# Attention products in plain float32, queries on partitions, inside a fused attention and MoE kernel

## The chip, the cores and the metric

The kernel runs on one core of one Trainium2 chip. The metric is device time of one execution in microseconds (us). Engines are named as the profile names them: PE (TensorE; PEld its weight loads), DVE (VectorE), ACT (ScalarE), POOL (GpSimd), SP (SyncE, which issues all DMAs).

## The reference

Sixteen heads (B = 2, H = 8) of 576 queries, D = 64, feed two dense stages over 1152 tokens:

```python
scores = scale * q @ k.T                        # causal
a = softmax(scores); local = a @ v              # the sum gets + 1e-9
q_p = where(q > 0, q, exp(q) - 1) + 1           # phi
mem_out = (q_p @ M_prev) / (q_p @ z_prev + 1e-6)
attn = g * mem_out + (1 - g) * local            # g = sigmoid(beta[h])
x = attn as (1152, 512)
x = ((x @ w1) * (x @ w2)) @ w3 @ w_out          # these four arrive as float64
out = sum over e of p[:, e] * (relu(x @ e_w1[e]) @ e_w2[e])   # 4 experts
```

## The kernel before, in words

Products are made accurate by splitting each operand into a high part rounded to the matrix type `float32r` and a low part (value minus high), and adding two or three float32r products (`PASSES`, line 29). A split costs a rounding copy (`hi`) and a subtraction (`lo`) on ACT, DVE or POOL (lines 75 to 82).

The program has four stretches. **Attention** goes head by head in slots of `run_slot(n)` (line 406): slot n holds the splits of head n+2 (`stage_h`), the scores and exponentials of head n+1 (`stage_a`), the transposes and value products of head n (`stage_b`), and for each pair of heads phi (`stage_pa`) and its transpose (`stage_pb`). The 576 queries are five tiles of 120 rows that start 114 apart; tile i sees 120, 234, 348, 462 or 576 keys. **Fills** run in the same slots: `wo_unit` converts w_out from float64 (8 units), `w_unit` converts w3 and multiplies it with w_out into W (16 units, tiles `w3s`, `wacc`), `b0` converts w1 and w2 and makes `ab` and `hT` for the first 576 tokens (16 units, tiles `ws`, `asb`), and `c_unit` multiplies `hT` by W (tiles `c`, `x2a`). Then comes **the second half of the tokens** (`b1`, lines 633 to 643: the same two steps), and last **the experts** (lines 663 to 711, products `d` and `o`).

In attention a score product is two float32r matmuls of 128 rows (both halves of a split stacked on partitions). DVE adds the mask and takes the row minimum (line 278), ACT makes the exponential and its row sum (line 284), POOL and ACT scale the probabilities by the gate over the sum (line 331). PE transposes the blocks of P (line 367), ACT and DVE split them (`ph`, `pl`), and the value and memory products accumulate with queries along columns (`xv`). phi is computed with queries on partitions, normalised, then transposed.

A float64 conversion (`from64`) reads a 512 KB raw tile, takes three DVE operations (lines 101, 102, 105) and one on ACT; raw tiles have two buffers, so load u+2 waits for unit u's last read.

What sets the order: the lists of times `PA_AT` to `B_AT` order the steps inside a slot, `WO_SLOTS`, `W_SLOTS` and `B_SLOTS` place the fills, and a scheduler then fixes one static order for each engine. Engines run their order strictly and wait on semaphores; the experts cannot start before `x2a` is there.

Of the kernel before, what the change touches and what calls it, by code (L numbers as in the profile page):

```python
# [10 lines left out]
U32 = mybir.dt.uint32  # L11
AF = mybir.ActivationFunctionType
# [20 lines left out]
def kernel(  # L33
    ctx: ExitStack,
    tc: tile.TileContext,
    q: bass.AP,
# [16 lines left out]
    B, H, S, D = q.shape  # L53
# [78 lines left out]
    raw_t, split_t, prob_t, xraw_t = {}, {}, {}, {}  # L132
    pair_t, pT_t = {}, {}
    ms2 = [A1.tile([P, 2, 2 * D], F32R, name=f"ms{i}") for i in range(2)]
    for t in ms2:
        nc.gpsimd.memset(r32(t), 0.0)

    def load_pair(p):

        b, h = divmod(2 * p, H)  # L140
        qn = A1.tile([RP, NQ, 2, D], F32, tag="qn", name=f"qn{p}")
        for x in range(2):
            src = q[b, h + x]
            nc.sync.dma_start(out=qn[:, :, x, :], in_=bass.AP(src.tensor, src.offset, [[D, RP], [R * D, NQ], [1, D]]))
        z = A1.tile([P, 2 * D], F32, tag="z", name=f"z{p}")
        nc.sync.dma_start(
            out=z, in_=z_prev[b, h : h + 2].rearrange("h d -> (h d)").unsqueeze(0).to_broadcast([P, 2 * D])
        )
        mr = A1.tile([P, D], F32, tag="mr", name=f"mr{p}")
        nc.sync.dma_start(out=mr, in_=M_prev[b, h : h + 2].rearrange("h d e -> (h d) e"))  # L150
        pair_t[p] = {"q": qn, "z": z, "m": mr}

    def load_head(n):

        b, h = divmod(n, H)
        ts = []
        for nm, src in (("q", qT), ("k", kT)):
            t = A1.tile([P, S], F32, tag=f"{nm}d", name=f"{nm}d{n}")
            for x in range(2):
                nc.sync.dma_start(out=t[x * D : (x + 1) * D, :], in_=src[b, h])  # L160
            ts.append(t)
        t = A2.tile([RP, NQ, D], F32, tag="vr", name=f"vr{n}")
        x = v[b, h]
        nc.sync.dma_start(out=t, in_=bass.AP(x.tensor, x.offset, [[D, RP], [R * D, NQ], [1, D]]))
        raw_t[n] = (*ts, t)

    def stage_pa(p):
# [3 lines left out]
        st = pair_t[p]
        h = 2 * p % H

        def phi_a():
            st["ex"] = ex = st["q"]
            st["phi"] = phi = A1.tile([RP, NQ, 2, D], F32, tag="phi", name=f"phi{p}")
            nc.scalar.activation(phi, st["q"], AF.Relu)
            nc.scalar.activation(ex, st["q"], AF.Exp)
            nc.vector.scalar_tensor_tensor(out=phi, in0=ex, scalar=1.0, in1=phi, op0=ALU.min, op1=ALU.add)

        def phi_b():
            ex, phi = (st[x].rearrange("p n h d -> p n (h d)") for x in ("ex", "phi"))
            nc.gpsimd.tensor_mul(ex, phi, st["z"][0:RP].unsqueeze(1).to_broadcast([RP, NQ, 2 * D]))
            m = ms2[p % 2]
            for x in range(2):
                o = slice(x * D, (x + 1) * D)
                hi_pool(m[o, x, 0:D], st["m"][o, :])
                lo_pool(m[o, x, D:], st["m"][o, :], m[o, x, 0:D])

        def phi_c():  # L190
            st["nrm"] = nrm = A1.tile([RP, NQ, 2], F32, tag="nrm", name=f"nrm{p}")
            nc.vector.reduce_sum(out=nrm, in_=st["ex"], axis=AX.X)
            nc.vector.scalar_tensor_tensor(
                out=nrm, in0=nrm, scalar=1e-6, in1=gm[0:RP, h : h + 2].unsqueeze(1).to_broadcast([RP, NQ, 2]),
                op0=ALU.add, op1=ALU.mult,
            )
            nc.vector.reciprocal(nrm, nrm)

        def phi_d():
            phi = st["phi"]  # L200
            nc.vector.tensor_mul(phi, phi, st["nrm"].unsqueeze(3).to_broadcast([RP, NQ, 2, D]))
# [7 lines left out]
    def stage_pb(p):  # L209

        if p >= B * H // 2:
            return []
        st = pair_t.pop(p)
        pT = A2.tile([P, 2, S], F32R, tag="pT", name=f"pT{p}")
        pT_t[2 * p] = pT_t[2 * p + 1] = pT

        def trans(c0, c1):
            def f():
                t0, t1 = q0[c0], q0[c1 - 1] + rows[c1 - 1]
                ps = psQ.tile([P, 512], F32, tag="Q", name=f"tp{c0}_{p}")[:, 0 : t1 - t0]  # L220
                for c in range(c0, c1):
                    w = rows[c]
                    nc.tensor.transpose(
                        ps[:, q0[c] - t0 : q0[c] - t0 + w], st["phi"][0:w, c].rearrange("p h d -> p (h d)"),
                        identF[0:w, 0:w],
                    )
                nc.scalar.copy(pT[:, 0, t0:t1], ps)
                lo_dve(pT[:, 1, t0:t1], ps, pT[:, 0, t0:t1])
            return f

        return [*zip(PB_AT, (trans(0, NQ - 1), trans(NQ - 1, NQ)))]

    def stage_h(n):

        if n >= B * H:
            return []
        qd, kd, vr = raw_t.pop(n)
        T = A2.tile([P, S], F32R, tag="T", name=f"T{n}")
        K = A2.tile([P, 2, S], F32R, tag="K", name=f"K{n}")
        vs = A2.tile([RP, NQ, 2 * D], F32R, tag="vs", name=f"vs{n}")  # L240
        split_t[n] = T, K, vs

        def fq():
            nc.scalar.copy(T, qd)
            lo_pool(T[D : 2 * D, :], qd[D : 2 * D, :], T[D : 2 * D, :])

        def fk():
            nc.scalar.copy(K[:, 0, :], kd)
            lo_pool(K[:, 1, :], kd, K[:, 0, :])

        def fv():
            hi_pool(vs[:, :, 0:D], vr)
            lo_pool(vs[:, :, D:], vr, vs[:, :, 0:D])

        def nothing():
            pass

        return [*zip(H_AT, (fk, fq, nothing, fv))]

    def stage_a(n):  # L260
# [61 lines left out]
        def norm():  # L322
            nc.vector.tensor_scalar(
                out=sm, in0=sm, scalar1=1e-9, scalar2=gl[0:RP, h : h + 1], op0=ALU.add, op1=ALU.mult
            )
            nc.vector.reciprocal(sm, sm)  # L326
            for i in range(NQ):
                if i == NQ - 1:
                    nc.scalar.activation(Pt[i], Pt[i], AF.Copy, scale=sm[:, i : i + 1])
                else:  # L330
                    nc.gpsimd.tensor_scalar(  # L331
                        out=Pt[i], in0=Pt[i], scalar1=sm[:, i : i + 1], scalar2=1.0, op0=ALU.mult, op1=ALU.mult
                    )

        return [
            *zip(A_AT, (s0, s1, s2, s3, norm))
        ]

    QC = 2 * R
    QH = ((0, QC), (QC, S))  # L340
    offs = [S * j - R * j * (j - 1) // 2 for j in range(NQ)]
# [405 lines left out]
```

## Time and profile before

| | us |
|---|---|
| median of 3 executions (802.13 to 914.89) | 803.92 |
| the profiled execution | 803.4 |
| its span, first to last instruction | 801.6 |
| PE busy in the span | 739.9 |
| DVE, POOL, ACT busy | 397.8, 354.3, 286.2 |

The shares of the whole span are means over stretches with different limits, so the stretches have to be read apart. A busy PE is an overlapping count: matmuls are pipelined, and the distance from one start to the next is what a matmul costs.

### The profile page before, as it was taken

What the parts mean: (1) busy time and instruction counts of PE and PEld (TensorE: products, weight loads), DVE (VectorE), ACT (ScalarE), POOL (GpSimd) and SP (SyncE); (2) the same over time, 40 slices, a digit from 0 to 9 for tenths busy, and PEclk for the clock granted to TensorE, in tenths of its full rate; (3) what the DMA queues carried; (4) which work ended last, traced back from release to release, by engine and by line L of the source; (5) the groups of instructions that cost most, each with busy time, mean ns of one, the idle gap of its engine ahead of it and who ended that gap; (6) DMA issues with size and microseconds to landing.
All of it is one profiled execution on the core that took longest, in us unless ns stands there. A gap on an engine that the chain in (4) does not pass through costs nothing.

```text
span 801.6 us, 11092 instructions
## 1 busy us (share of the span) xinstructions
PE 739.9 (92%) x4120; PEld 655.6 (82%) x4120; DVE 397.8 (50%) x786; ACT 286.2 (36%) x639; POOL 354.3 (44%) x362
## 2 busy tenths in 40 slices
PE   3768688899899999989999999999999999999998
PEld 2656577679798999889988988889888898888986
DVE  5999988989999962756331211212112121121211
ACT  5777667667777733343220101201012010120100
POOL 7998987686754325723392009500095001600000
PEclk9666899989999999999999999999999999999999
DMA  7634445454342322531141003200033000201010
GB/s 195 180 115 139 136 140 151 127 152 133 117 118 86 105 80 80 170 106 54 28 130 54 1 1 119 92 1 1 1 121 90 1 1 1 66 0 40 14 40 26
DMA packets 65477, 64.37 MB, mean 80 GB/s; under 512 B 25360, under 2 KB 50960, under 8 KB 65424
## 3 DMA queue, kind: packets, MB, share of 16 engines
q1 hardware_dynamic: 65424, 63.67, 26.6%
q8 instruction: 32, 0.52, 0.3%
q14 instruction: 21, 0.17, 0.1%
HBM read 61.30 MB, written 2.36 MB: 79 GB/s over the span
## 4 chain that ended last, share of the span: by engine, by line
PE 63%; DVE 17%; POOL 6%; DMA 6%; issue 5%; ACT 3%; SPq 0%; DVEq 0%; POOLq 0%; ACTq 0%
PE d L673 25%; PE o L690 25%; PE ab L508 4%; PE c L568 4%; PE wacc L456 2%; DMA wr<-in_moe_w_dram 2%; DVE tu L102 2%; DMA w3r<-in_moe_w3T_dram 2%; DVE tf L105 2%; DVE P L278 2%; POOL P L331 2%; DVE pl L82 2%; PE xv L391 1%; DMA qd<-in_qT_dram 1%; PE pt L367 1%
## 5 line engine op out<-in xcount | busy, mean ns | idle before, releaser
L690 PE MATMUL o<-el,he 128*128 128x512 f32 x864 | 201.3, 393 | 0.0
L690 PEld LDWEIGHTS o<-el,he 128*128 128x128 f32 x864 | 161.9, 188 | 36.4
L679 ACT ACTIVATE he<-d 128x512 fp32r<-128x512 f32 (+2 forms) x96 | 47.2, 491 | 342.4 <-PE d L673 339.9
L76 POOL TENSOR_SCALAR el<-rel 128x512 fp32r<-128x512 f32 x64 | 40.4, 636 | 210.8 <-PE d L673 187.8
L680 DVE SCALAR_TENSOR_TENSOR he<-d,he 128x512 fp32r<-128x512 f32 (+2 forms) x96 | 53.5, 558 | 147.8 <-ACT he L679 147.8
L508 PE MATMUL ab<-xT,ws 128*128 128x288 f32 x768 | 115.7, 302 | 1.9 <-DVE asb L555 1.6
L673 PE MATMUL d<-x2b,el 128*128 128x384 f32 (+1 forms) x768 | 113.7, 309 | 0.0
L673 PEld LDWEIGHTS d<-x2b,el 128*128 128x128 f32 x768 | 113.1, 189 | 0.7
L508 PEld LDWEIGHTS ab<-xT,ws 128*128 128x128 f32 x768 | 107.5, 193 | 3.6 <-DVE asb L555 1.6
L673 PE MATMUL d<-x2a,el 128*128 128x512 f32 x384 | 89.6, 394 | 0.0
L673 PEld LDWEIGHTS d<-x2a,el 128*128 128x128 f32 x384 | 72.1, 188 | 16.7
L79 POOL TENSOR_TENSOR el<-rel,el 128x512 fp32r<-128x512 f32 x64 | 83.5, 1319 | 1.6
L699 DVE SCALAR_TENSOR_TENSOR acc<-o,pr,acc 128x512 f32<-128x512 f32 x27 | 20.3, 751 | 125.7 <-PE o L690 125.7
L273 PE MATMUL sc<-K,T 128*120 128x120 f32 (+2 forms) x192 | 49.7, 382 | 18.4 <-POOL K L79 10.9
L456 PE MATMUL wacc<-wo,w3s 128*128 128x512 f32 x192 | 55.4, 439 | 6.3 <-DVE W L82 6.3
L568 PE MATMUL c<-hT,W 128*128 128x288 f32 x384 | 56.0, 297 | 3.3 <-DVE hT L82 3.1
L331 POOL TENSOR_SCALAR P<-P,sm 120x120 f32<-120x120 f32 (+1 forms) x64 | 48.8, 778 | 20.6 <-DVE sm L326 13.2
L568 PEld LDWEIGHTS c<-hT,W 128*128 128x128 f32 x384 | 52.1, 188 | 4.3 <-DVE hT L82 3.8
L273 PEld LDWEIGHTS sc<-K,T 128*120 128x120 f32 x192 | 34.6, 225 | 23.9 <-POOL K L79 11.4
L284 ACT ACTIVATE P<-P,mn 120x120 f32<-120x120 f32 (+4 forms) x80 | 46.6, 583 | 19.4 <-DVE mn L278 19.0
L456 PEld LDWEIGHTS wacc<-wo,w3s 128*128 128x128 f32 x192 | 40.0, 215 | 15.4 <-DVE W L82 7.0
L367 PE MATMUL pt<-identF,P 114*120 114x114 f32 (+1 forms) x240 | 43.8, 297 | 8.5 <-POOL P L331 5.5
(89 smaller groups left out, 966.7 us busy)
## 6 DMA issues: line engine op xcount, KB each, us to landing
wr<-in_moe_w_dram SPq DMA_DIRECT2D x32, 512.0 KB, 3.4
rel<-in_moe_w_dram SPq DMA_DIRECT2D x64, 256.0 KB, 2.7
w3r<-in_moe_w3T_dram SPq DMA_DIRECT2D x16, 512.0 KB, 3.5
qd<-in_qT_dram SPq DMA_DIRECT2D x32, 144.0 KB, 3.7
kd<-in_kT_dram SPq DMA_DIRECT2D x32, 144.0 KB, 3.1
wor<-in_moe_w_out_dram SPq DMA_DIRECT2D x8, 512.0 KB, 3.7
vr<-in_v_dram SPq DMA_DIRECT2D x16, 150.0 KB, 3.0
qn<-in_q_dram SPq DMA_DIRECT2D x16, 150.0 KB, 3.8
```

The lines of the kernel that those rows point to most:

```text
L79: nc.gpsimd.tensor_sub(dst, src, r32(hi))
L273: nc.tensor.matmul(ps_ap, lhsT=T[:, q0[i] : q0[i] + RP], rhs=K[:, 1 - m, k0:k1], start=(m == 0), stop=(m == 1))
L284: nc.scalar.activation(Pt[i], Pt[i], AF.Exp, bias=mn[:, i : i + 1], scale=-1.0, accum_out=sm[:, i : i + 1])
L331: nc.gpsimd.tensor_scalar(out=Pt[i], in0=Pt[i], scalar1=sm[:, i : i + 1], scalar2=1.0, op0=ALU.mult, op1=ALU.mult)
L367: nc.tensor.transpose(pt[:, o - c0 : o - c0 + rows[i]], Pt[i][0 : rows[i], q0[j] : q0[j] + RP], identF[0 : rows[i], 0 : rows[i]],)
L456: nc.tensor.matmul(wacc[t], lhsT=w3s[u][:, a, c, :], rhs=wo[4 * g + c][:, bb, :], start=(g == 0 and c == 0 and x == 0), stop=(g == 1 and c ...
L508: nc.tensor.matmul(ps[:, 0:HS], lhsT=self.ws[u][:, wi, kk, :], rhs=xT[b, kk][:, xi, a * HS : (a + 1) * HS], start=(n == 0), stop=(n == 3 * ...
L568: nc.tensor.matmul(st["ps"][:, 0:HS], lhsT=Wt[kk][:, wi, d * P : (d + 1) * P], rhs=hT[kk][:, xi, a * HS : (a + 1) * HS], start=(kk == 0 an ...
L673: nc.tensor.matmul(ps, lhsT=ew1[m // 4 * 4 + kk][:, wi, m % 4 * P : (m % 4 + 1) * P], rhs=rhs[:, xi, :], start=(n == 0), stop=(n == 3 * KD ...
L679: nc.scalar.activation(ht[:, 0, :], ps, AF.Relu)
L680: nc.vector.scalar_tensor_tensor(out=ht[:, 1, :], in0=ps, scalar=0.0, in1=r32(ht[:, 0, :]), op0=ALU.max, op1=ALU.subtract,)
L690: nc.tensor.matmul(po, lhsT=hs[kk][:, xi, tt * P : (tt + 1) * P], rhs=ew2[kk][:, wi, :], start=(n == 0), stop=(n == 3 * KF - 1),)
```

## The change

The attention products become plain float32 instead of sums of float32r products, with queries on partitions in the results. Scores: one product of 64 rows (`qd`, `kd` as loaded, two heads of a pair on the two halves of the partitions). Values and memory: the transposed block of P (or phi, now computed on the transposed q) is the stationary operand, and v (or M) is the moving one with a column of ones (or z) beside it, so the row sum comes out as column 65; the result is scaled by gate over sum on DVE (`out_of`) and the two parts are added on POOL. The finished pair is transposed and split into `xT`. The splits of q, k, v, P, M and phi are gone, as are the scaling of P and the plain `q` input. In `from64` the shift on DVE becomes an ACT operation on the upper 16 bits of the low word. The `hi` copies of w_out, w3 and b0's weights move from ACT to POOL, b0's `lo` from DVE to POOL. The lists of times are new, and the fills start earlier: `wo_unit` from slot -0.8, `w_unit` in slots 1 to 8, `b0` in 8 to 13, `c_unit` in 13 to 16.

```diff
-WO_SLOTS = (0, 0, 0, 1, 1, 1, 2, 2)
-W_SLOTS, B_SLOTS = (3.0, 10.5), (10.5, 15.0)
+WO_SLOTS = (-0.8, -0.5, -0.2, 0.1, 0.3, 0.5, 0.7, 0.9)
+W_SLOTS, B_SLOTS, C_SLOTS = (1.0, 8.0), (8.0, 13.0), (13.0, 16.0)
 def from64(raw, tmp, nm):
+        nc.scalar.activation(u, raw.bitcast(U16)[..., 1], AF.Copy, scale=2.0**-13, bias=2.0**-14 - 0.5)
         nc.scalar.activation(t, hi.bitcast(F32), AF.Copy, scale=2.0**-112)
-        nc.vector.tensor_scalar(out=u, in0=lo, scalar1=29, scalar2=None, op0=ALU.logical_shift_right)
 def load_pair(p):
...
+            t = A2.tile([P, S], F32, tag=f"{nm}d", name=f"{nm}d{p}")
+            nc.sync.dma_start(out=t, in_=src[b, h : h + 2].rearrange("h d s -> (h d) s"))
 def stage_phi(p):
...
+            nc.gpsimd.tensor_scalar(out=phi, in0=qd, scalar1=0.0, scalar2=1.0, op0=ALU.max, op1=ALU.mult)
+            nc.scalar.activation(ex, qd, AF.Exp)
+            nc.vector.scalar_tensor_tensor(out=phi, in0=ex, scalar=1.0, in1=phi, op0=ALU.min, op1=ALU.add)
 def stage_a(n):
...
-            for m in range(2):
-                nc.tensor.matmul(
-                    ps_ap, lhsT=T[:, q0[i] : q0[i] + RP], rhs=K[:, 1 - m, k0:k1], start=(m == 0), stop=(m == 1)
-                )
+            nc.tensor.matmul(ps_ap, lhsT=qd[:, q0[i] : q0[i] + RP], rhs=kd[:, k0:k1], start=True, stop=True)
-                Pt[i], Pt[i], AF.Exp, bias=mn[:, i : i + 1], scale=-1.0, accum_out=sm[:, i : i + 1]
+            nc.scalar.activation(Pt[i], Pt[i], AF.Exp, bias=mn[:, i : i + 1], scale=-1.0)
-        def norm():
...
 def stage_b(n):
         def trans(g):
...
-                nc.scalar.copy(ph[:, c0:c1], pt[:, : c1 - c0])
-                lo_dve(pl[:, c0:c1], pt[:, : c1 - c0], ph[:, c0:c1])
+                nc.scalar.copy(t, ps)
+        def pv(*tiles):
...
+                        nc.tensor.matmul(
+                            st["a"][:, i, :], lhsT=pt[i, j][0 : rows[j]], rhs=vn[0 : rows[j], j, :],
+                            start=(j == 0), stop=(j == i),
+                        )
+        def mem():
+            ps = psS.tile([P, 512], F32, tag="S", name=f"b{n}")[0:RP, 0 : NQ * (D + 1)]
+            m = ps.rearrange("p (i d) -> p i d", d=D + 1)
+            for i in range(NQ):
+                nc.tensor.matmul(
+                    m[:, i, :], lhsT=phi[o : o + D, q0[i] : q0[i] + RP], rhs=mz[o : o + D, p, :], start=True, stop=True
+                )
+            out_of(m, 1, 1e-6, gm)
+        def out_of(ps, x, eps, g):
+            nc.vector.tensor_scalar(
+                out=rr[:, x, :], in0=ps[:, :, D], scalar1=eps, scalar2=g[0:RP, h : h + 1], op0=ALU.add, op1=ALU.mult
+            )
+            nc.vector.reciprocal(rr[:, x, :], rr[:, x, :])
...
+            nc.vector.tensor_mul(dst, ps[:, :, 0:D], rr[:, x, :].unsqueeze(2).to_broadcast([RP, NQ, D]))
+        def join():
+            out_of(st["a"], 0, 1e-9, gl)
+            nc.gpsimd.tensor_add(xq[:, :, n % 2, :], xq[:, :, n % 2, :], st["m"])
         def fin():
...
+                nc.scalar.copy(xt[:, 0, t0:t1], ps)
+                lo_dve(xt[:, 1, t0:t1], ps, xt[:, 0, t0:t1])
 def wo_unit(c):
-            nc.scalar.copy(wo[c][:, 0, :], f)
+            hi_pool(wo[c][:, 0, :], f)
 def w_conv(u):
-        nc.scalar.copy(w3s[u][:, 0], f)
+        hi_pool(w3s[u][:, 0], f)
-    b0 = BUnits(0, nc.scalar.copy, lo_dve)
+    b0 = BUnits(0, hi_pool, lo_pool)
```

The order moves in two places that matter here. On SP at the start stand the loads of w_out and what lies between them (`wor` is raw w_out; `qn`, `qd`, `kd`, `vr`, `v` are inputs of attention, `z` and `mr` the memory). Before:

```order
L429 DMA wor_291<-in_moe_w_out_dram 128x1024
L429 DMA wor_357<-in_moe_w_out_dram 128x1024
L146 DMA z_189<-in_z_prev_dram 128x128
L144 DMA qn_186<-in_q_dram 120x5x64
L160 DMA qd_178<-in_qT_dram 64x576 x2
L144 DMA qn_186<-in_q_dram 120x5x64
L160 DMA kd_181<-in_kT_dram 64x576 x2
L164 DMA vr_261<-in_v_dram 120x5x64
L429 DMA wor_403<-in_moe_w_out_dram 128x1024
```

And with the change:

```order
L340 DMA wor_165<-in_moe_w_out_dram 128x1024
L340 DMA wor_185<-in_moe_w_out_dram 128x1024
L152 DMA v_109<-in_v_dram 120x5x64
L340 DMA wor_199<-in_moe_w_out_dram 128x1024
L340 DMA wor_232<-in_moe_w_out_dram 128x1024
L340 DMA wor_272<-in_moe_w_out_dram 128x1024
L340 DMA wor_299<-in_moe_w_out_dram 128x1024
L340 DMA wor_326<-in_moe_w_out_dram 128x1024
L145 DMA qd_346<-in_qT_dram 128x576
L145 DMA kd_348<-in_kT_dram 128x576
L340 DMA wor_336<-in_moe_w_out_dram 128x1024
```

Nine loads now stand ahead of the first `wor` where there were seventeen, and three stand between the first and the eighth where there were 25.

On PE, the first product of W (`wacc`; `sc` are scores, `pt` transposes of P, `a` value products, `tp` phi's transposes). Before:

```order
L273 MATMUL sc_4_879<-K_586,T_585 120x462 x2
L273 MATMUL sc_4_889<-K_586,T_585 120x512 x2
L367 MATMUL pt_3_799<-identF,P_3_588 120x114
L367 MATMUL pt_3_809<-identF,P_3_592 120x120
L367 MATMUL pt_3_799<-identF,P_3_589 120x114
L367 MATMUL pt_3_809<-identF,P_3_589 120x114
L223 MATMUL tp_2_795<-identF,phi_600 128x120
L456 MATMUL wacc_779<-wo_116,w3s_765 128x512
```

And with the change:

```order
L188 MATMUL sc_2_474<-kd_144,qd_142 120x462
L270 MATMUL a_453<-v_108,pT_1_409 120x65 x2
L188 MATMUL sc_2_510<-kd_144,qd_142 120x512
L270 MATMUL a_453<-v_108,pT_1_432 120x65 x4
L258 MATMUL pt_2_556<-identF,P_2_351 120x120
L270 MATMUL a_453<-v_108,pT_1_460 120x65
L367 MATMUL wacc_393<-wo_119,w3s_370 128x512
L270 MATMUL a_453<-v_108,pT_1_460 120x65
L367 MATMUL wacc_393<-wo_119,w3s_370 128x512 x2
L367 MATMUL wacc_393<-wo_120,w3s_370 128x512 x3
```

W's first product stood behind the scores of head 4 and transposes of head 3; now it stands behind the scores of head 2 and nearly all value products of head 1.

## Rows read from the trace of the kernel before

**Rows 1.** Busy time by stretch: PE, PEld, DVE, ACT, POOL, clock, DMA share, GB/s.

```profile
0.00:75.00 75.00, 46.63 (x181) 38.24 (x182) 61.67 (x135) 50.98 (x115) 65.83 (x75) 0.73 0.58 161
75.00:284.00 209.00, 184.96 (x1129) 165.31 (x1128) 194.57 (x422) 148.71 (x343) 141.96 (x141) 0.93 0.43 126
284.00:313.00 29.00, 28.85 (x220) 28.85 (x221) 10.62 (x20) 7.48 (x18) 6.52 (x8) 1.00 0.21 68
313.00:397.00 84.00, 78.81 (x578) 76.75 (x577) 48.33 (x74) 31.51 (x68) 38.31 (x33) 1.00 0.27 89
397.00:802.00 405.00, 400.70 (x2016) 346.41 (x2014) 82.61 (x137) 47.55 (x97) 101.72 (x109) 1.00 0.13 41
```

**Rows 2.** Timeline of PE: start, length; first W product, second half begins, experts begin.

```profile
74.65 0.74 PE L456 MATMUL wacc<-wo,w3s 128*128 128x512 f32 x1
...
312.87 8.10 PE L508 MATMUL ab<-xT,ws 128*128 128x288 f32 x60
...
396.79 13.46 PE L673 MATMUL d<-x2a,el 128*128 128x512 f32 x57
```

**Rows 3.** Timeline of PE in attention, warm: start and length of merged matmuls.

```profile
262.52 0.59 PE L273 MATMUL sc<-K,T 128*120 128x120 f32 x4
262.95 0.32 PE L391 MATMUL xv<-ph,vs 114*128 114x348 f32 x1
...
267.23 0.95 PE L367 MATMUL pt<-identF,P 114*120 114x114 f32 x8
267.95 0.70 PE L273 MATMUL sc<-K,T 128*120 128x348 f32 x4
268.48 0.47 PE L386 MATMUL xv<-pT,ms 128*128 128x228 f32 x2
268.79 3.35 PE L508 MATMUL ab<-xT,ws 128*128 128x288 f32 x24
271.97 0.27 PE L391 MATMUL xv<-ph,vs 114*128 114x228 f32 x1
...
277.18 0.48 PE L386 MATMUL xv<-pT,ms 128*128 128x348 f32 x2
...
279.19 1.79 PE L508 MATMUL ab<-xT,ws 128*128 128x288 f32 x12
```

**Rows 4.** Timeline of weight loads, same stretch: the loads of eight transposes, two short products.

```profile
266.63 0.19 PEld L391 LDWEIGHTS xv<-ph,vs 120*128 120x128 f32 x1
266.74 0.19 PEld L391 LDWEIGHTS xv<-pl,vs 120*128 120x128 f32 x1
...
267.10 0.86 PEld L367 LDWEIGHTS pt<-identF,P 114*120 114x120 f32 x8
```

**Rows 5.** Chain that ended last, one piece: start, length.

```profile
396.95 22.40 PE d L673 x96
```

**Rows 6.** Groups of DVE up to 400 us: busy us, mean ns, idle before.

```profile
L82 DVE TENSOR_TENSOR pl<-pt,ph 120x456 fp32r<-120x456 f32 (+1 forms) x64 | 37.4, 597 | 3.9 <-ACT ph L371 3.7
L101 DVE TENSOR_SCALAR tu<-wr 128x512 uint32<-128x512 uint32 x32 | 18.0, 561 | 12.8 <-DMA wr<-in_moe_w_dram 12.7
L398 DVE TENSOR_TENSOR xraw<-xv,xl 64x228 f32<-64x228 f32 (+1 forms) x32 | 14.2, 443 | 3.3 <-ACT xl L397 2.8
```

**Rows 7.** Group of ACT up to 400 us: busy us, mean ns, idle before.

```profile
L100 ACT ACTIVATE tf<-wr 128x512 f32<-128x512 f32 x32 | 21.7, 677 | 11.6 <-POOL ws L79 7.5 <-DMA wr<-in_moe_w_dram 2.3 <-DVE ws L82 1.7
```

**Rows 8.** Groups of POOL up to 400 us: busy us, mean ns, idle before.

```profile
L331 POOL TENSOR_SCALAR P<-P,sm 120x120 f32<-120x120 f32 (+1 forms) x64 | 48.8, 778 | 20.6 <-DVE sm L326 13.2 <-ACT hT L556 7.2
...
L79 POOL TENSOR_TENSOR ws<-tf,ws 128x512 fp32r<-128x512 f32 x16 | 22.7, 1421 | 39.7 <-ACT ws L498 39.7
```

**Rows 9.** SP's DMA issues: start, length; first and last w_out, first w3.

```profile
12.18 0.89 SPq L429 DMA_DIRECT2D wor<-in_moe_w_out_dram  x2
...
51.14 0.36 SPq L429 DMA_DIRECT2D wor<-in_moe_w_out_dram  x1
...
58.88 0.38 SPq L440 DMA_DIRECT2D w3r<-in_moe_w3T_dram  x1
```

More of the change, by code (lines that the diff above doesn't have):

```diff
@@ L129 @@
     psT = attn.enter_context(tc.tile_pool(name="psT", bufs=2, space=PSUM))
[L132 to L136, printed above, removed]
+    qk_t, v_t, phi_t, prob_t, xq_t = {}, {}, {}, {}, {}
+    mz = A1.tile([P, B * H // 2, D + 1], F32, name="mz")
+    v3 = [A1.tile([RP, NQ, D + 1], F32, name=f"v{i}") for i in range(3)]
+    for t in v3:
+        nc.gpsimd.memset(t[:, :, D : D + 1], 1.0)
@@ L138, in load_pair @@
     def load_pair(p):
         b, h = divmod(2 * p, H)
[L141 to L147, printed above, removed]
-        )
@@ L161, in load_head @@
+            nc.sync.dma_start(out=t, in_=src[b, h : h + 2].rearrange("h d s -> (h d) s"))
             ts.append(t)
[L162 to L167, printed above, removed]
+        qk_t[p] = ts
+    def load_head(n):
+        x = v[divmod(n, H)]
+        nc.sync.dma_start(
+            out=v3[n % 3][:, :, 0:D], in_=bass.AP(x.tensor, x.offset, [[D, RP], [R * D, NQ], [1, D]])
+        )
@@ L169, in stage_pa, with stage_phi @@
+    def stage_phi(p):
         if p >= B * H // 2:
             return []
[L171 to L178, printed above, removed]
-            nc.vector.scalar_tensor_tensor(out=phi, in0=ex, scalar=1.0, in1=phi, op0=ALU.min, op1=ALU.add)
[L181 to L201, printed above, removed]
@@ L205 @@
+        return [*zip(PHI_AT, (f0, f1))]
     q0 = [R * i for i in range(NQ)]
@@ L207 @@
     rows = [R] * (NQ - 1) + [RP]
[L209 to L258, printed above, removed]
     def stage_a(n):
@@ L320, in s3 @@
             expo(4)
-        def norm():
[L323 to L341, printed above, removed]
-    PW = offs[-1] + RP
-    blocks, chunks = [], [[0, 0]]
-    for j in range(NQ):
-        for i in range(j, NQ):
-            o = offs[j] + q0[i] - q0[j]
-            if o + rows[i] - chunks[-1][0] > 512:
-                chunks.append([o, o])
-            chunks[-1][1] = o + rows[i]
-            blocks.append((o, i, j))
+        return [*zip(A_AT, (s0, s1, s2, s3))]
@@ L352, in stage_b @@
+    NB = 4
+    blocks = [(i, j) for i in range(NQ) for j in range(i + 1)]
     def stage_b(n):
         b, h = divmod(n, H)
-        Pt, vs = prob_t.pop(n)
-        pT, ms = pT_t.pop(n), ms2[n // 2 % 2][:, n % 2, :]
-        ph = A1.tile([RP, PW], F32R, tag="ph", name=f"ph{n}")
-        pl = A1.tile([RP, PW], F32R, tag="pl", name=f"pl{n}")
+        p, o = n // 2, n % 2 * D
+        Pt, vn, phi = prob_t.pop(n), v3[n % 3], phi_t[p]
+        st = {}
+        pt = {}
+        if n % 2 == 0:
+            xq_t[0] = A2.tile([RP, NQ, 2, D], F32, tag="xq", name=f"xq{p}")
+        xq = xq_t[0]
+        rr = A2.tile([RP, 2, NQ], F32, tag="rr", name=f"rr{n}")
@@ L361, in trans @@
         def trans(g):
             def f():
-                c0, c1 = chunks[g]
-                pt = psT.tile([P, 512], F32, tag="T", name=f"pt{g}_{n}")[0:RP]
-                for o, i, j in blocks:
-                    if c0 <= o < c1:
-                        nc.tensor.transpose(
-                            pt[:, o - c0 : o - c0 + rows[i]], Pt[i][0 : rows[i], q0[j] : q0[j] + RP],
-                            identF[0 : rows[i], 0 : rows[i]],
-                        )
-                nc.scalar.copy(ph[:, c0:c1], pt[:, : c1 - c0])
@@ L401, in fin @@
-        def fin():
-            if h % 2 == 1:
-                xt = xT[b, h // 2]
-                hi_pool(xt[:, 0, :], xr)
-                lo_pool(xt[:, 1, :], xr, xt[:, 0, :])
+                mine = blocks[g * NB : (g + 1) * NB]
+                ps = psT.tile([P, 512], F32, tag="T", name=f"pt{g}_{n}")[0:RP, 0 : RP * len(mine)]
+                t = A2.tile([RP, RP * len(mine)], F32, tag=f"pt{g}", name=f"pT{g}_{n}")
+                for x, (i, j) in enumerate(mine):
+                    sl = slice(x * RP, (x + 1) * RP)
+                    nc.tensor.transpose(ps[:, sl], Pt[i][:, q0[j] : q0[j] + RP], identF[0:RP, 0:RP])
+                    pt[i, j] = t[:, sl]
@@ new lines, in f @@
+                nc.scalar.copy(t, ps)
+            return f
+        def pv(*tiles):
+            def f():
+                if "a" not in st:
+                    ps = psQ.tile([P, 512], F32, tag="Q", name=f"a{n}")[0:RP, 0 : NQ * (D + 1)]
+                    st["a"] = ps.rearrange("p (i d) -> p i d", d=D + 1)
+                for i in tiles:
+                    for j in range(i + 1):
+                        nc.tensor.matmul(
+                            st["a"][:, i, :], lhsT=pt[i, j][0 : rows[j]], rhs=vn[0 : rows[j], j, :],
+                            start=(j == 0), stop=(j == i),
+                        )
+            return f
@@ new lines, in join @@
+        def join():
+            out_of(st["a"], 0, 1e-9, gl)
+            nc.gpsimd.tensor_add(xq[:, :, n % 2, :], xq[:, :, n % 2, :], st["m"])
+        def fin():
+            if n % 2 == 0:
+                return
+            xt = xT[b, h // 2]
+            for c0, c1 in ((0, NQ - 1), (NQ - 1, NQ)):
+                t0, t1 = q0[c0], q0[c1 - 1] + rows[c1 - 1]
+                ps = psS.tile([P, 512], F32, tag="S", name=f"x{c0}_{p}")[:, 0 : t1 - t0]
+                for c in range(c0, c1):
+                    w = rows[c]
+                    nc.tensor.transpose(
+                        ps[:, q0[c] - t0 : q0[c] - t0 + w], xq[0:w, c].rearrange("p h d -> p (h d)"), identF[0:w, 0:w]
+                    )
+                nc.scalar.copy(xt[:, 0, t0:t1], ps)
+                lo_dve(xt[:, 1, t0:t1], ps, xt[:, 0, t0:t1])
```

105 lines of the change are left out of this document (39 added, 66 removed).

## The prediction, made before the run

> **What bounds the kernel now.** I read the stretches first [rows 1]. From 397 us PE is busy 400.7 of 405 us and the change touches nothing there. From 284 to 397 us PE is busy 107.7 of 113 us (95.3%), so it bounds there too. From 75 to 284 us it does not: DVE is busy 194.6 of 209 us (93%), PE 185.0 (88.5%) in a count that overlaps, and PE's clock is 0.93, which means it fell to 1.2 GHz now and then. From 0 to 75 us nothing is full and PE's clock is 0.73. So before 284 us DVE sets the pace, with a slow start in front: the first product of W comes at 74.65 us, the second half of the tokens starts at 312.87 us, the experts at 396.79 us [rows 2]. What the change can give or take lies before 312.87 us, plus a little in the 84 us behind; the last 405 us stay.
>
> The costs of PE have to be read as distances between starts [rows 3, 4]. At the high clock 24 products of 288 columns take 271.97 - 268.79 = 3.18 us, 0.1325 each. Eight transposes of P go by in 0.72 us by the matmuls and 0.86 us by their loads, so 0.090 to 0.108; I take 0.10. Two short products of 120 columns have their loads 0.11 apart: below some 120 columns the weight load is the price. 512 columns cost 22.40/96 = 0.233 [rows 5].
>
> **PE, removed.** 192 score products: 0.43/4 = 0.108 for 120 and 234 columns, 0.53/4 = 0.133 for 348 and 64 [rows 3], 0.222 for 462 and 512 (0.233 times 487/512); mean 0.154, so 29.6 us. 288 value and memory products: 14 in 279.19 - 277.18 = 2.01 us, 0.144 each, so 41.4 us. Together 71.0 us.
>
> **PE, added.** 96 score products, 240 value products, 80 memory products. As built, a plain float32 product is two weight loads with a MATMUL each (low and high half of the weights), which rules out the lower bound, one float32r record per product. The only plain float32 records in the trace are the transposes: 0.10 for 114 columns, 0.88 ns a column, and that is my price of a record, with the load's 0.10 as its floor. A head's scores: 0.106 + 0.206 + 0.306 + 0.10 + 0.407 + 0.451 = 1.58 us, twice, 3.15 us; 16 heads 50.4 us. The 320 others have 65 moving columns (0.057 us) behind a load of 120: the floor holds, 640 x 0.10 = 64.0 us. Together 114.4 us: **43.4 us more PE time** than before. The transposes stay 280 (28 us). Bounds of this price: 0.057 us per record of values (27.5 us less) if a plain load is shorter than a transpose lets us see, and twice the stream (59 us more).
>
> What would upset this price is a transpose that tells too little, since load and stream may be equally long in it. The Trainium skill, "TensorE: Matmul & The Clock Gate", section "Terms", says that the transpose mode is four times faster for FP32; an estimate by it is four transposes per product where I take two, so some 62 us on the time. No row here shows which holds. The other doubt is whether loads hide: if they did not, every added record would cost load plus stream, 192 x 0.10 + 640 x 0.057 = 56 us more. The trace speaks against it: 24 products with a load each stand 0.1325 apart, where a load alone takes 0.11. The same page, section "Part 3: Packing small matmuls — row/col tiling", says that a weight load overlaps running matmuls only when it addresses other rows of the array, which would make it so here; the trace disagrees, by those 0.1325 us.
>
> **DVE.** Off in 0 to 284 us: the low halves of P (37.4 us), the sum of the halves (14.2) and 40 shifts of 0.56 (22.4) [rows 6], and smaller splits and norms that I leave out of the bound. Added: 32 chains of three operations, each at most the 0.443 of the xraw row, so at most 43 us. DVE's 256 us [rows 1] become at most 225, in truth nearer 170. **ACT** gains 40 conversions of 0.677 [rows 7], 27 us on 200 us; it loses the splits and row sums, so even the bound of 227 stays below PE. **POOL** loses at least the scaling of P (48.8 us) and gains 40 copies of at most 0.78, 16 low halves and 16 additions of at most 1.42 [rows 8], some 77 us on 208: at most 236. So none of the three reaches PE's sum, at the costs above and with 0.233 for W and 0.1325 for `ab` and `c`: scores 50.4, values 64.0, transposes 28.0, W 192 x 0.233 = 44.8, `ab` 384 x 0.1325 = 50.9, `c` 25.4: 263.5 us to the end of `c` (220 before). **PE becomes the bound of the stretch**, and the cover of everything costed at nothing is PE's own work.
>
> **The start.** Before, the eight w_out loads are issued from 12.18 to 51.14 us, 5.6 us a unit, and w3 at 58.88 [rows 9]. Now nine loads stand ahead, at 0.45 us an issue [rows 9] with some waiting: first w_out near 6 us. Two raw buffers still chain the units, with a shorter DVE part and three loads between in place of 25: I take 4.5 us a unit, the eighth at 38, w3 at 41, landed and converted for the first product of W at 48 us. With the old 5.6 it is 56; with less waiting 43. Ahead of that product stand on PE the scores of heads 0 to 2 and transposes, memory and values of heads 0 and 1: 9.5 + 3.1 + 2.0 + 6.0 = 20.6 us at 2.4 GHz, 41 us at 1.2, which fits in front of 48 at either clock. The new `mz` load in 4-byte pieces has no row; it is first needed by the memory products of head 0 and has this slack as cover, at most the 8 us above if not.
>
> **The sum.** From 48 us PE has 263.5 - 20.6 = 242.9 us to do. Its share where it bounds now is 95.3% [rows 1]; so 254.9 us, and `c` ends at 302.9 us where it ended at 312.9. In the 84 us behind, DVE loses 16 shifts (9 of its 48.3 us) and PE idles 5.2 us; I take 2 us off, between 0 and 5. At the seam the last pair's transposes must wait for a chain of DVE and POOL with 27 products of `ab` (3.6 us) as cover; 0 to 2 us. Span 801.6 - 10.0 - 2.0 = 789.6; the execution lies 1.8 us over its span (803.4), so **791 us**. The median of the runs shown, 803.92, stands 0.5 over the profiled execution, which I neglect.
>
> **Rivals.** (1) *Plain loads are shorter than 0.10 us.* Then value records cost their 65 columns, 27.5 us less, 28.9 at 95.3%: 762 us. For it: in a transpose stream and load tie, so 0.10 is only an upper limit of the load. Against: the float32r loads of 120-row blocks stand 0.11 apart [rows 4]. Chance 0.20.
> (2) *Waits take DVE's place.* The attention chain now runs PE, DVE, ACT, PE, ACT, PE, DVE, POOL per head, ACT converts in the same queue as the exponentials, and a conversion that waits for a late w3 tile holds the copies of P behind it. Then PE keeps the share of 75 to 284 us, 88.5%: 48 + 242.9/0.885 = 322.5, 20 us later, 811 us. For it: with DVE as the bound, that stretch kept DVE at 93% and no more [rows 1]. Against: nothing but PE is near full any more. Chance 0.19.
> (3) *A plain product costs twice my price, slower.* A record streams at 1.76 ns a column: scores 50.4 us more, values (0.114 against 0.10) 9 more, 62 us at 95.3%: 853 us. It decides from a small excess: 27 us more, 23% over my 114.4, is enough to be slower by 2%. For it: no row shows a plain product that is not a transpose. Against: two records per product already double the float32r price per column (0.233/512 = 0.46 ns), and 0.88 is close to twice that. Chance 0.11: 0.09 for a slower stream, 0.02 for loads that do not hide (58 us at 95.3%, 849 us). The Trainium skill's rules above, "Terms" for the first and "Part 3" for the second, are the two forms of this rival.
>
> **How the numbers follow.** Forecast 0.50: shares of 92 to 97% and the start at 43 to 56 us make it 783 to 803. Measured differences under 2% count as none here: faster is below 787, slower above 819.5. Faster: rival 1 and the part of the forecast from 97% up, 0.20 + 0.14. Slower: rival 3 and a little of rival 2, 0.12. The rest, 0.54, is no difference. The range must leave out 2 in 10: rival 3 and the ends of rivals 1 and 2; so 763 to 815 us.
>
> **What would show it.** Right: rows for plain products come twice per product; score records of 512 columns near 0.45 us and value records near 0.10 apart; PE over 95% busy from 50 to 300 us with the clock near 1.00; DVE under 75% there; first product of W near 48 us; `ab` of the second half near 301 us; the experts' 405 us as before. Wrong: value records at 0.06 (rival 1), PE waits on ACT or DVE of some 2 us per slot (rival 2), 512 columns at 0.9 us or loads in series (rival 3), or the first product of W still after 60 us.

## The result, and the profile after

The changed kernel takes **810.89 us** (median of 10 runs, 810.10 to 813.14) against 804.72 for the kernel before on the same chip: ratio 1.0082, 95% interval 1.0063 to 1.0101. The forecast was 791, 1.6% faster. It is 0.8% slower, a small loss that the interval separates from nothing, though it is under the 2% from which the prediction counts a difference. The ratio leaves out the one execution of 914.89 us of the kernel before, which was in a slower state of the chip. The profiled execution has a span of 808.7 us.

First the busy time by stretch, cut where the changed kernel changes its pace (columns as in [rows 1]):

```profile
0.00:47.00 47.00, 41.13 (x144) 28.26 (x144) 26.92 (x65) 25.49 (x47) 26.40 (x33) 1.00 0.62 174
47.00:75.00 28.00, 22.34 (x116) 18.79 (x116) 14.59 (x30) 13.30 (x25) 10.90 (x11) 0.88 0.42 129
75.00:284.00 209.00, 209.00 (x1358) 170.49 (x1357) 120.13 (x323) 110.59 (x217) 74.08 (x71) 1.00 0.32 96
284.00:320.00 36.00, 36.00 (x272) 32.94 (x271) 9.33 (x31) 10.82 (x22) 1.74 (x2) 1.00 0.00 1
320.00:404.00 84.00, 79.32 (x579) 76.74 (x578) 44.25 (x66) 37.65 (x81) 40.27 (x34) 1.00 0.31 98
404.00:809.00 405.00, 400.85 (x2017) 346.35 (x2016) 82.74 (x137) 47.57 (x97) 102.07 (x109) 1.00 0.14 41
```

From 75 to 284 us DVE fell from 194.6 [rows 1] to 120.1 us (57%), the clock rose from 0.93 to 1.00, and PE is busy all 209 us. PE has become the bound, as forecast, and it has more to do than was added up. The 1.00 of the first row is not a reading: the trace has no granted clock before 51.5 us, and until then PE's records stand as far apart as at half clock (512 columns of `wacc` 0.427 us from 48.4 to 51.4, 0.23 from 51.7 on, where 1.00 is granted). The 0.73 of [rows 1] is no full reading either: that trace has a granted clock from 24.0 us on. The timeline of PE gives the marks that answer to [rows 2], and its one long wait:

```profile
46.99 0.77 PE L367 MATMUL wacc<-wo,w3s 128*128 128x512 f32 x1
...
61.60 1.65 PE L258 MATMUL pt<-identF,P 120*120 120x120 f32 x7 [5.66 <-ACT pT L260]
...
319.38 1.35 PE L419 MATMUL ab<-xT,ws 128*128 128x288 f32 x9
...
403.95 1.32 PE L584 MATMUL d<-x2a,el 128*128 128x512 f32 x5
```

The first product of W comes 27.7 us earlier than before (forecast 48, now 46.99). From there to the second half it takes 272.4 us, where it took 238.2 before and the forecast had 254.9. The second half takes 84.6 (83.9 before, 82 forecast), the experts the same 405. So the loss is one stretch: 27.7 us won at the start, 34.2 lost behind it.

**Where it goes.** Two rows of the timeline of PE and three of its weight loads, at one place where a score product of 512 columns stands between value products and `ab` (start, length; two records per plain float32 product):

```profile
199.36 1.17 PE L270 MATMUL a<-v,pT 114*120 114x65 f32 x10
200.45 1.12 PE L188 MATMUL sc<-kd,qd 64*120 64x512 f32 x2
201.50 0.67 PE L419 MATMUL ab<-xT,ws 128*128 128x288 f32 x3
```

```profile
200.45 0.28 PEld L188 LDWEIGHTS sc<-kd,qd 64*120 64x120 f32 x2
201.50 0.57 PEld L419 LDWEIGHTS ab<-xT,ws 128*128 128x128 f32 x4 [0.77 <-issue]
```

The load of `ab` starts at 201.50. The second score record began at 200.98 in the trace and has 512 columns, 0.43 us by the first experiment below; so the load waited until that stream was over, 0.77 us behind the load before it, with "issue" as its releaser: nothing that the profile knows held it. The score's own load did the same: it starts 0.20 us after the last value record, where loads of value records come 0.10 us apart. The mark of the two handovers is the `64*120` in the row: it is the height and width of the weights, 64 rows for scores and memory, 114 to 128 for all else.

Taken over all handovers from 70 to 300 us (three distances between starts around each, less the streams of the three records, medians): 114 to 128 rows to 64, **0.16 us** (57 of them); 64 to 114 to 128, **0.19 us** (57); between two kinds that are both 114 to 128 rows high, -0.01 (105). The order of the built program has 139 changes of height, 122 of them between 47 and 319 us.

The scores of one head and the memory products of the other lie on the two different halves, and a change between them costs nothing: -0.03 where scores go on behind memory products (5). At the same five places PE even works on both at once:

```profile
74.18 0.94 PE L280 MATMUL b<-mz,phi 64*120 64x65 f32 x7
74.86 0.55 PE L188 MATMUL sc<-kd,qd 64*120 64x348 f32 x1
74.96 0.47 PE L280 MATMUL b<-mz,phi 64*120 64x65 f32 x3
75.25 1.44 PE L188 MATMUL sc<-kd,qd 64*120 64x348 f32 x5
```

A score record of 348 columns (0.293 us elsewhere) starts at 74.86, and the memory records beside it go on 0.105 us apart as if it were not there. That takes 0.29 us off at each of these places.

**Theory A**: each change of height costs PE 0.16 to 0.19 us, some 0.35 in and out, because the load behind it does not start under the running stream; 139 changes are 22 to 26 us (the expectations below round this to 27). **Rival B**: the plain float32 product shows its loads whatever its rows. **Rival C**: waits for other engines set the pace (the prediction's second rival).

### The profile page after: what moved, and what is told of

It is laid out like the page before. It is cut to its first block, busy times and chain, and to the rows that moved or that the text cites. A ratio compares the mean times of both kernels' runs of the same rounds, so it can differ in the third digit from the quotient of the medians.

```text
span 808.7 us, 11140 instructions
## 1 busy us (share of the span) xinstructions
PE 788.6 (98%) x4472; PEld 673.6 (83%) x4472; DVE 298.0 (37%) x650; ACT 245.4 (30%) x487; POOL 255.5 (32%) x259
## 4 chain that ended last, share of the span: by engine, by line
PE 86%; DMA 6%; POOL 3%; ACT 2%; DVE 2%; SPq 1%; issue 1%; DVEq 0%; POOLq 0%; ACTq 0%
PE d L584 25%; PE o L601 25%; PE ab L419 9%; PE sc L188 6%; PE a L270 6%; PE c L477 5%; PE wacc L367 5%; PE pt L258 3%; DMA w3r<-in_moe_w3T_dram 2%; DMA wor<-in_moe_w_out_dram 2%; PE b L280 2%; POOL el L77 1%; DMA wr<-in_moe_w_dram 1%; POOL ws L77 1%; POOL el L74 1%
## 5 line engine op out<-in xcount | busy, mean ns | idle before, releaser
L419 PE MATMUL ab<-xT,ws 128*128 128x288 f32 x768 | 112.9, 299 | 2.5 <-POOL ws L77 1.7
L419 PEld LDWEIGHTS ab<-xT,ws 128*128 128x128 f32 x768 | 104.0, 188 | 7.8 <-issue 4.0
L188 PE MATMUL sc<-kd,qd 64*120 64x120 f32 (+2 forms) x192 | 72.1, 496 | 5.9 <-DMA kd<-in_kT_dram 5.9
L270 PEld LDWEIGHTS a<-v,pT 114*120 114x120 f32 (+1 forms) x480 | 62.7, 200 | 14.5 <-issue 11.7
L270 PE MATMUL a<-v,pT 114*120 114x65 f32 (+1 forms) x480 | 66.5, 282 | 0.0
L477 PE MATMUL c<-hT,W 128*128 128x288 f32 x384 | 60.3, 302 | 2.2 <-DVE hT L80 1.9
L77 POOL TENSOR_TENSOR ws<-tf,ws 128x512 fp32r<-128x512 f32 x32 | 42.9, 1342 | 38.4 <-ACT ws L409 37.2
L258 PE MATMUL pt<-identF,P 120*120 120x120 f32 x240 | 41.7, 293 | 5.7 <-ACT pT L260 5.7
```

The costliest lines, as they stand in the source:

```text
L77: nc.gpsimd.tensor_sub(dst, src, r32(hi))
L188: nc.tensor.matmul(ps_ap, lhsT=qd[:, q0[i] : q0[i] + RP], rhs=kd[:, k0:k1], start=True, stop=True)
L258: nc.tensor.transpose(ps[:, sl], Pt[i][:, q0[j] : q0[j] + RP], identF[0:RP, 0:RP])
L270: nc.tensor.matmul(st["a"][:, i, :], lhsT=pt[i, j][0 : rows[j]], rhs=vn[0 : rows[j], j, :], start=(j == 0), stop=(j == i),)
L419: nc.tensor.matmul(ps[:, 0:HS], lhsT=self.ws[u][:, wi, kk, :], rhs=xT[b, kk][:, xi, a * HS : (a + 1) * HS], start=(n == 0), stop=(n == 3 * ...
L477: nc.tensor.matmul(st["ps"][:, 0:HS], lhsT=Wt[kk][:, wi, d * P : (d + 1) * P], rhs=hT[kk][:, xi, a * HS : (a + 1) * HS], start=(kk == 0 an ...
```

## The experiments

The kernel before, timed again beside every experiment, took 803.7 to 804.0 us (804.7 beside the changed kernel), so a difference to the changed kernel below 1 us is not read as one.

**1. All products on 128 rows.** q of each head lies in a tile whose other half is zero, and mz has zeros in the other head's rows, so that the product over 128 rows gives the same sums. (q and M then come in two loads each, and phi is made half by half.)

```diff
+            nc.sync.dma_start(out=qp[x][x * D : (x + 1) * D, :], in_=qT[b, h + x])
...
-        qd, kd = (t[o : o + D] for t in qk_t[n // 2])
+        qp, kd = qk_t[n // 2]
+        qd = qp[n % 2]
...
-                    m[:, i, :], lhsT=phi[o : o + D, q0[i] : q0[i] + RP], rhs=mz[o : o + D, p, :], start=True, stop=True
+                    m[:, i, :], lhsT=phi[:, q0[i] : q0[i] + RP], rhs=mz[:, n, :], start=True, stop=True
```

> Changed alone: score and memory products run over all 128 rows (q of each head in a tile whose other 64 rows are zero, mz with zeros in the other head's rows); columns and order of the work stay. Theory A (each change between a product on 64 rows and one on 114 to 128 rows costs about 0.19 us on PE, because its weight load starts only when the stream before it has ended; 139 such changes): 27 us less, 784 us, c ends near 294 us, and a score record of 512 columns is followed at 0.43 to 0.45 us. Rival B (the plain float32 product itself shows its loads, whatever the rows): 811 us, records at 0.52 us as before. Rival C (waits on other engines set the pace): 805 to 811.

Measured 782.01 us, ratio to before 0.9743 (0.9704 to 0.9783). The same place in the rows of the loads, then of PE:

```profile
236.06 0.29 PEld L196 LDWEIGHTS sc<-kd,qz 128*120 128x120 f32 x2
236.60 0.19 PEld L427 LDWEIGHTS ab<-xT,ws 128*128 128x128 f32 x1 [0.25 <-issue]
```

```profile
236.12 1.07 PE L196 MATMUL sc<-kd,qz 128*120 128x512 f32 x2
236.63 0.96 PE L427 MATMUL ab<-xT,ws 128*128 128x288 f32 x3
...
289.43 1.35 PE L427 MATMUL ab<-xT,ws 128*128 128x288 f32 x9
```

The load of `ab` now starts at 236.60, as the second score record begins, not when it ends. The handovers that cost 0.16 and 0.19 us cost -0.02 and -0.02, and a score record of 512 columns is followed at 0.434 us where it was 0.52 to 0.53. The second half begins at 289.4, 30 us earlier. Twice the rows cost nothing. Rival B falls (811 expected), and so does C: PE is idle for 14.8 us up to 290 us here, and was for 11.5 us up to 320 us in the changed kernel, so the gain is not idle time.

That A's 27 us came out at 28.9 is in part luck, for the handovers are not the whole of it. Priced by what records of each kind stand apart in this run, the work up to the second half is the same 263 us in both kernels. On top of it the changed kernel has 19.6 us at its 61 stays on 64 rows behind 47 us, 0.32 each, and some 25 us for work at half clock (until 51.5 us, and from 61.6 to 65.1). Here the full clock is granted from 10.3 us, and half clock comes back only from 34.2 to 47.9: some 9 us with the time before 10.3. So, as estimates from these distances, handovers are worth 20 us and the clock 16, and 6 are lost again in waits and at the start, where W's first product comes at 60.1 us (47.0 in the changed kernel) with more of attention ahead of it. Whether the rows or the new order brought the clock up was not tried by itself.

The handover alone shows from 140 us to the second half, where both kernels have the full clock and neither waits: 14.8 of 179 us are left over in the changed kernel, 0.34 for each of 43 stays, and 0.7 of 149 us here.

**2. Fewer changes of height, same products.** Only the score steps' places in the slot move.

```diff
-A_AT = (0.1, 0.3, 0.5, 0.7)
+A_AT = (0.1, 0.1, 0.5, 0.5)
```

> Changed alone: the positions of the four score steps in a slot, two and two together, so that PE changes between 64-row products and the others 111 times in place of 139. Theory A: 28 x 0.19 = 5 us less, 805 to 806 us. Rival B (price of the plain product): no change, 811. Rival C (waits): slower by some us, since three score buffers are asked for closer together.

Measured 803.90 us, 7.0 below the changed kernel, with 111 changes in place of 139. Nothing of the work is different, only what stands beside what, and PE's one long wait is in both traces (5.66 and 5.9 us). C expected a loss. A expected 5 us; that the rest comes from scores beside memory products fits, since in this trace ten memory records from 137.7 to 138.7 us have four score records among them (two of 348 columns, two of 64) and still stand 0.105 apart after the first; it was not tried by itself.

**3 and 4. The cost by itself.** A product with no use, one for each of the 96 groups of `d` in the experts' stage, where PE never waits: in the program it stands in the middle of the group.

```diff
...
+                        if n == 6:
+                            nc.tensor.matmul(
+                                dm[:, 0:288], lhsT=ew1[m // 4 * 4][0:64, 0, 0:128],
+                                rhs=x2a[0][0:64, 0, 0:288], start=True, stop=True,
+                            )
```

The fourth kernel has 128 rows and plain float32 operands in its place.

> Added alone, in the experts' stage, where PE is full: 96 float32r products of 288 columns on 64 rows, one in the middle of each group of 12 products on 128 rows (result unused). Theory A: 96 x (0.133 + 0.39) = 50 us more, 861 us. Rival B (only plain float32 pays): 96 x 0.133 = 13 us more, 824 us.

> Added alone at the same 96 places: plain float32 products of 288 columns on 128 rows (result unused). Theory A: two records of 288 columns at 0.83 ns, 96 x 0.48 = 46 us more, 857 us, no extra at the change of kind. Rival B: 96 x (0.48 + 0.39) = 83 us more, 894 us.

Measured 853.64 and 856.59 us (one execution each), 42.8 and 45.7 over the changed kernel. PE in the kernel with 64 rows, then the load of its added product, then the loads in the one with plain float32 on 128 rows:

```profile
514.37 0.63 PE L585 MATMUL d<-x2a,el 128*128 128x512 f32 x2
514.92 0.40 PE L591 MATMUL dm<-x2a,el 64*128 64x288 f32 x1
515.25 0.74 PE L585 MATMUL d<-x2a,el 128*128 128x512 f32 x2
```

```profile
514.92 0.18 PEld L591 LDWEIGHTS dm<-x2a,el 64*128 64x128 f32 x1 [0.36 <-issue]
```

```profile
516.96 0.19 PEld L585 LDWEIGHTS d<-x2a,el 128*128 128x128 f32 x1
517.19 0.42 PEld L591 LDWEIGHTS dm<-x2a,el 128*128 128x128 f32 x2
517.66 0.89 PEld L585 LDWEIGHTS d<-x2a,el 128*128 128x128 f32 x4
```

A float32r product of 64 rows alone among 128-row products adds 0.52 us (medians 0.524, 0.526, 0.520 for neighbours of 512, 384 and 256 columns): 0.133 for itself and 0.39 for going in and out. The neighbours' width does not matter. 72 of the 96 stand alone among `d`; those of the first expert were put ahead of the experts, in groups of 14, 9 and 1, which explains 42.8 in place of 50: 72 x 0.524 + 24 x 0.133 + 3 x 0.39 = 42.1. The plain product of 128 rows adds 0.486, which is its two records of 0.243 and no more; the load behind it, at 517.66, waits for nothing. So the height costs, not the number format. This is Theory A by itself, without attention.

**5. The early start alone,** on the kernel before.

```diff
-WO_SLOTS = (0, 0, 0, 1, 1, 1, 2, 2)
-W_SLOTS, B_SLOTS = (3.0, 10.5), (10.5, 15.0)
+WO_SLOTS = (-0.8, -0.5, -0.2, 0.1, 0.3, 0.5, 0.7, 0.9)
+W_SLOTS, B_SLOTS = (1.5, 9.5), (9.5, 14.5)
...
```

> The kernel before with the changed kernel's early w_out loads alone (eight units from slot -0.8 to 0.9, W and ab one slot to one and a half earlier; attention untouched). Theory A (DVE paces the stretch up to 284 us, so only its idle time in the start can be won): 5 to 15 us less than before, 790 to 799 us. Rival (the chain of waits of each head sets the pace, not the start): 802 to 806 us.

Measured 803.88 us, ratio 0.9994 (0.9975 to 1.0013): my expectation missed. SP's issues show why:

```profile
12.52 0.90 SPq L429 DMA_DIRECT2D wor<-in_moe_w_out_dram  x2
...
50.76 0.46 SPq L429 DMA_DIRECT2D wor<-in_moe_w_out_dram  x1
60.61 0.39 SPq L440 DMA_DIRECT2D w3r<-in_moe_w3T_dram  x1
```

They are where they were [rows 9]. The list hardly moved them in SP's order: the same seventeen loads are issued ahead of the first. And where SP waits longest at w_out, it waits for DVE's last read of a raw tile (8.3 us in three waits), so an earlier place does not start the load. The 27.7 us at the start do not come from the list alone; that they come from the attention edits, which empty DVE and POOL, or from these with the list, is what remains, and was not tried by itself.

**6 and 7. The shift on ACT alone:** added to the kernel before, and undone in the changed one.

```diff
-        nc.vector.tensor_scalar(out=u, in0=lo, scalar1=29, scalar2=None, op0=ALU.logical_shift_right)
+        nc.scalar.activation(u, raw.bitcast(U16)[..., 1], AF.Copy, scale=2.0**-13, bias=2.0**-14 - 0.5)
```

> The kernel before with one edit of the change alone: the shifted low words of the f64 weights come from ScalarE, not from DVE (40 operations of 0.56 us on DVE become 40 of 0.68 on ACT ahead of 313 us). Theory A (DVE paces the stretch): 8 to 20 us less, 785 to 796 us. Rival (ACT's queue, which already delays the copies of P, takes over): 800 to 812 us.

> The changed kernel with that edit undone: the shift is back on DVE. Theory A (PE is full from 64 us on, DVE 57% busy): no change from 64 us on; ACT is freer in the start, so the 5.7 us wait of PE on ACT near 58 us may go: 804 to 812 us. Rival (DVE still matters): 815 us or more.

On the kernel before, 792.82 us, ratio 0.9862 (0.9834 to 0.9890): 11 us from this one edit, where DVE was the bound. Undone in the changed kernel, 818.55, 7.7 more than it; I had expected none. The stretches of that run, cut where the second half begins (321 us, 319 with the edit):

```profile
0.00:321.00 321.00, 309.06 (x1877) 250.15 (x1878) 193.52 (x493) 134.44 (x262) 119.38 (x117) 0.99 0.33 99
321.00:412.00 91.00, 82.34 (x583) 79.98 (x583) 52.26 (x76) 32.42 (x73) 40.63 (x34) 0.96 0.28 90
```

The first half is as expected, within 1.5 us. The second half takes 91 us in place of 84.6, with its clock at 0.96 and PE waiting 4.9 us, in three waits, for DVE's read of a finished `ab`. An engine that is 57% busy over the stretch still decides at those places.

**8. Wider value products.** 96 moving columns in place of 65.

```diff
-v3 = [A1.tile([RP, NQ, D + 1], F32, name=f"v{i}") for i in range(3)]
+v3 = [A1.tile([RP, NQ, 96], F32, name=f"v{i}") for i in range(3)]
...
```

> The changed kernel with 96 moving columns in each value product in place of 65 (the further 31 are columns of ones, unused). Theory A (the weight load of 120 columns sets the 0.105 us from record to record, so 0.080 us of columns fit under it): 811 us, records still 0.105 apart. Rival (a fixed 0.05 us at each record on top of the columns): 480 x 31 x 0.83 ns = 12 us more, 823 us, records 0.131 apart.

Measured 803.75 us (one execution). Six value records ahead of `ab`, with 65 columns in the changed kernel and with 96 here:

```profile
197.12 0.75 PE L270 MATMUL a<-v,pT 114*120 114x65 f32 x6
197.67 1.85 PE L419 MATMUL ab<-xT,ws 128*128 128x288 f32 x12
```

```profile
190.42 0.77 PE L270 MATMUL a<-v,pT 114*120 114x96 f32 x6
190.97 1.85 PE L419 MATMUL ab<-xT,ws 128*128 128x288 f32 x12
```

0.55 us both times; the median distance is 0.105 us with 65 and with 96 columns. The load is the price. The 7 us less do not come from the records, which stand where they stood: the planner's order came out otherwise, the wait of 5.66 us near 58 us is not there, and the full clock is granted at 25.5 us for the first time, not at 51.5.

**9 and 10. The memory products alone on 128 rows; three raw buffers.** The ninth has the mz edit of the first kernel without its q edit; the tenth has one edit at each load of f64 weights:

```diff
-            r = pf.tile([P, DM, 2], U32, tag="raw", name=f"wor{c}")
+            r = pf.tile([P, DM, 2], U32, tag="raw", name=f"wor{c}", bufs=3)
```

> The changed kernel with the memory products alone on 128 rows (zeros in the other head's rows of mz); the scores stay on 64 rows, 115 changes of tile height in place of 139. Theory A: 24 x 0.19 = 5 us less, 806 us. If the memory products on 64 rows were harmless: 811.

> The changed kernel with three raw buffers for the f64 weights in place of two. If the chain of raw buffers makes ACT wait for w3 tiles with copies of P behind it (the 5.7 us wait of PE near 58 us): the wait goes, 804 to 806 us. If the wait comes from the transfers themselves: 809 to 812 us.

Measured 800.86 and 806.47 us. The ninth saves 10.0, twice what I expected: 24 changes fewer are 4.6, and the wait of 5.66 us is not in its trace either (PE is busy all 262 us from 48 to 310). The tenth saves 4.4: in place of that wait PE has one of 2.3 and one of 1.1.

**11 and 12. Both together,** and with the pairing of the second experiment.

> Scores and memory products on 128 rows and three raw buffers: PE is idle or at half clock for some 15 us of the first 60 us in the kernel on 128 rows alone; three buffers give back at most 8 of them: 774 to 782 us.

> The same with the score steps two and two together. With no 64-row products left, Theory A says that the pairing saves nothing more: within 2 us of the kernel on 128 rows with three raw buffers. If pairing helps by waits and not by tile height, as much as it did on 64 rows: 7 us less.

Measured **774.75 us**, ratio to before 0.9648 (0.9625 to 0.9671), and 775.19. The pairing, worth 7 us where heights change, is worth nothing where they don't, which is what A says (there are no halves left to work side by side either, so this does not part the two). The eleventh kernel beats both kernels: PE is busy 225.7 of 228 us between the first product of W (here at 55.6, with more of attention ahead of it) and the second half, which begins at 283.3.

## Why the prediction was wrong

**Right: what bounds.** PE became the bound, DVE went to 57% (said: under 75%), the clock was 1.00 from 65 us on, plain products have two records each, value records stand 0.105 us apart (said 0.10, by the load, which the eighth experiment shows), the experts are unchanged. That W starts at 47.0 (said 48) is in part luck: w3 was issued at 36.3 (said 41), and from there to the first product it took 10.7 us (said 7).

**Wrong: the step "PE, added", 114.4 us.** It priced each new record by its columns or its load, and nothing for what stands beside it. The records themselves were priced well: with all products on 128 rows scores and values cost what was said (0.434 us for 512 columns where I had 0.451; 0.243 for 288 columns is 0.84 ns a column where I had 0.88). What was missing is the handover: 122 changes of height between 47 and 319 us at 0.16 to 0.19. The forecast had 254.9 us there, 12 of them as idle time; it took 272.4. Work of 242.9, handovers of 20 to 24 (19.6 by the distances, or 0.39 for each of 61 stays), one wait of 5.66, and 4 for work at half clock (until 51.5 us, and from the end of the wait at 61.6 until 65.1) make 272 to 277. The idle time was sized about right, by the wait and the clock; the handovers stood at nothing.

I had the doubt in hand and answered it from rows that could not decide it. "The trace speaks against it: 24 products with a load each stand 0.1325 apart" is true of neighbours of one height, and the kernel before has no other: its T, ms and vs fill 114 to 128 rows. That the new scores have 64 stood in the diff. The rows had no price for it, so it needed a bound from below and above, as any unseen operation; I gave it to a rival with chance 0.02 and a price for every load, 849 us, where it holds only at changes of height.

The Trainium skill has the rule: "TensorEngine Tiling (Array Packing)", section "Tiling Modes", says that a change of the tiling mode, other than a change of the tile within one, drains TensorE, and counts two tiles of 64 rows as a mode of their own. The runs agree on both points and give the price: 0.39 us in and out in the third experiment, nothing between the two halves. I had weighed another rule of the Trainium skill, in "TensorE: Matmul & The Clock Gate", section "Part 3: Packing small matmuls — row/col tiling", by which a load overlaps running matmuls only on other rows; the first experiment disagrees, where the load of `ab` at 236.60 is hidden under a stream on the same rows.

**The rivals.** The second (waits take DVE's place, 811 us) gave the number that came, and not the reason: it had PE at 88.5%, and PE is at 100% from 75 us on. Its mechanism showed once, in the 5.66 us near 58 us, where a conversion on ACT waited for a w3 tile with the copies of P behind it (timeline of ACT, changed kernel):

```profile
59.40 0.66 ACT L99 ACTIVATE tu_l<-w3r 128x512 uint32<-128x512 uint16 x1 [3.47 <-DMA w3r<-in_moe_w3T_dram]
...
60.98 1.03 ACT L260 COPY pT<-pt 120x480 f32<-120x480 f32 x2
```

The first rival (shorter loads) is refuted by the 0.105 us, the third's slower stream by 0.84 ns a column.

**The second half.** I took 2 us off; it took 0.7 more. The edit that should give them does (3.8 us in the sixth experiment, 83.9 to 80.1; 6 in the seventh), so something else in the change takes as much back. PE waits there for POOL's `ws` (1.7 us) and DVE's `hT` (1.9), and the last pair's `x` transposes now stand at its beginning. Which of these it is was not tried and stays open.

## What to carry to other kernels

Write the height in rows beside every kind of product on PE and count the changes in the order: a product on half the rows costs a fifth of a microsecond each time PE goes in, and again out. Filling the other rows with zeros costs no time on PE and removes it. It also gives up what the two halves can do side by side (0.29 us at each of five places here); whether an order that pairs them throughout would beat the zeros was not tried. And a row that shows something hidden shows it for its own neighbours only; where the change makes a neighbourhood that no row has, it needs bounds of its own.

## What was not expected of the hardware

- A change between weights of 64 rows and of 114 to 128 costs 0.16 to 0.19 us in attention (0.39 in and out among products of 128 rows in the third experiment, whatever the neighbours' width); a change between the two halves costs nothing.
- Products of 64 rows on the two halves stream at the same time: memory records stand 0.105 us apart with a score record of 348 columns (0.293 us alone) running beside them.
- The full clock is granted at 10.2 to 11.5 us in the three kernels with scores and memory products on 128 rows. In the changed kernel, where PE works without a pause from 5.9 us on, it is granted at 51.5, and in six of the seven others with scores on 64 rows at 49.7 to 51.9 (25.5 in the eighth experiment). What decides it was not tried.
- A plain float32 product streams as two records of 0.84 ns a column each (0.243 us for 288 columns), 1.69 ns in all, against 0.46 for float32r with 512 columns [rows 5], 3.7 times as much. The Trainium skill, "FP8 and Floating Point Precision", section "TensorE Precision Notes", counts four passes for it, which agrees.
- Between 65 and 96 moving columns, plain products with a load of 120 columns keep the same distance, 0.105 us.
